# Two attention heads' blocks on one core: a periodic loop with its output group and VectorE's small work at one place in 16 steps

## Chip, cores, metric

One core of a Trainium2 chip runs the kernel. The metric is the device time in microseconds, as the median of several runs; before the change it is 1823.55 us (three runs, 1822.85 to 1823.87). "The loop" below is the main loop over 512 steps, in which nearly all the attention of block B is done.

## The reference

Two independent attention blocks over 2048 rows of 640 numbers, with 32 heads of 20 columns each; their outputs are put side by side. In A a row attends to eight keys, itself and seven before it, two apart; in B to all 2048.

```python
def _A_ref(x, wqkv, wo):
    ...
    logits = jnp.einsum("bhsd,bhswd->bhsw", q, kg) * scale
    logits = jnp.where(mask[None, None, :, :], logits, -1e9)
    attn = _softmax(logits, axis=-1)
    o = jnp.einsum("bhsw,bhswd->bhsd", attn, vg)
    return (lambda x, *d: x.transpose(*d))(o, 0, 2, 1, 3).reshape(B, S, D) @ wo

def _B_ref(x, wqkv, wo):
    ...
    scores = jnp.einsum("bhqd,bhkd->bhqk", q, k) * (Dh ** -0.5)
    p = _softmax(scores, axis=-1)
    o = jnp.einsum("bhqk,bhkd->bhqd", p, v)
    return (lambda x, *d: x.transpose(*d))(o, 0, 2, 1, 3).reshape(B, S, D) @ wo

return jnp.concatenate([a, b], axis=-1)
```

## The kernel before

The program is written out by Python in a fixed order: each engine has a wrapper `InOrder` (line 48) whose instructions keep the order in which they are written, so all work of an engine stands in one line of the profile, L60. A counter `now` is moved on by `tick()`, and `after(n, fn, ...)` puts work n ticks later. Ahead of the loop stand the projections of A and of B and the value groups of B; behind it the last output groups.

**Block B in the loop.** Four heads are worked on together (`g`, 8 of them), with 512 queries at a time (`qc`, 4); a unit `u` is one (g, qc), and it has 16 steps, one for each 128 keys. A step has four score matmuls ("s"; two heads in a plane `pl`, one in each row half `r` of TensorE's array), each followed by an exponential on ScalarE out of its PSUM bank (`e<-ps_st`), and the product of the exponentials of two steps earlier with V ("P", `b_pv`, four heads side by side in one bank). Two steps of P are summed in the bank; then ScalarE copies it (`more<-ps_st`), and GpSimd adds it to the unit's sum (`braw`).

The exponentials need the maximum of each query's row, which is taken out of the scores themselves by two additional rows of the operands. So the scores are computed a second time, transposed and 24 steps ahead (`LEAD`), as "m" matmuls, and VectorE takes the maximum out of PSUM (`mx<-ps_st`): a single one over 512 columns or a double one over two neighbouring banks, 1024 columns. A step has four m matmuls. At a unit's end `max_rows` reduces the sixteen columns on VectorE, transposes them, splits them on GpSimd and takes them through DRAM into the operand q. `normalize`, also at a unit's end, takes the sums through DRAM, a reciprocal on VectorE (`sm`), back through DRAM, and a product on GpSimd.

In the trace, an s matmul has 62 rows (`ps_st<-bq,bk 62*128`: a head's 20 columns three times, as high and low parts, and the two rows of the maximum), an m matmul 60 (`ps_st<-bk,bq 60*128`), and P is `ps_st<-e,vb`.

**The order of a pair of steps.** `b_pair` writes two steps at a time: P, then three couples of matmuls through `b_two`, P, and five couples, in the order P, s+m, m+m, s+s; P, s+m, m+m; s+s, s+m, s+m. Each couple uses both row halves of the array. m+m is read by one double maximum, the m of an s+m by a single one: two doubles and four singles per pair. Between the second and the third part of every third pair, an output group may stand. PSUM has eight banks (`psb`). Once the loop has begun, `one` and `two` choose a bank for each matmul when the program is written, out of the program's own account of when each bank has been read (`read_at`, `pe.us`, `act.us`, `dve.us`).

**Block A in the loop.** GpSimd does A's windows in 128 units (`a_attention`): per tile of 128 rows four units of scores, then `a_softmax` (a maximum and a reciprocal on VectorE, `am`, an exponential on ScalarE, the rest on GpSimd), then four units with V. In the loop a unit is written at 8 of 30 steps. A finished tile is turned by `a_turn`: VectorE transposes five blocks (`turn`), one a step, which go through DRAM and come back (`back`); `turn_parts` splits them on GpSimd. `a_out` then multiplies the tile by A's output weights: two output groups per tile, each of fifteen matmuls (`ps_st<-ww,aot`) into one bank, which ScalarE copies out (`ro`). 32 such groups stand in the loop. `fill` holds the output groups of B, which come up near the end.

Of the kernel before, what the change touches and what calls it, by code (L numbers as in the profile page):

```python
# [21 lines left out]
KC = 5  # L22
# [42 lines left out]
def attention_pair(ctx, tc, xa, wqk_a, wv_a, wo_a, xb, wqk_b, wv_b, wo_b, oa, ob):  # L65
# [16 lines left out]
    loop = [None]  # L82

# [14 lines left out]
    read_at = []  # L98

    def bank():  # L100
# [259 lines left out]

    def a_softmax(t):

        _, L, _ = a_t[t]
        if t % (NT // 2) == 0:
# [8 lines left out]
        yield  # L373
# [5 lines left out]
        yield  # L379
        dve.reciprocal(m[:, 0], m[:, 0])  # L380
        yield
        pool(L, L, m[:, 0].unsqueeze(1).to_broadcast([128, WIN, H]), ALU.mult)
# [17 lines left out]
    def a_attention():  # L400
        for n in range(2):
            a_fetch(n)
        soft = {}
        for n, (t, c) in enumerate(UNITS):
            a_fetch(n + 2)
            for g in soft.values():
                next(g, None)
            if c == 4:
                for _ in soft.pop(t):
# [12 lines left out]
            next_a[0] = n + 1  # L422
            yield
# [165 lines left out]
    def max_rows(m4, m1, q, qc):  # L589
# [5 lines left out]
        def turn():  # L595

            dve.transpose(raw, m1)

# [12 lines left out]
        t = odd(1)  # L611
        after(t, dve.tensor_reduce, m1[:, :16], m4.rearrange("p r a c -> p (r a) c"), AX.X, ALU.max)
        after(t, turn)
        after(t + 1, parts)
        after(t + 3, store)
        after(t + 4, load)

    def normalize(raw, g, c0, t, then):
# [9 lines left out]
        def out():  # L628
            for j in range(GH):
                r0 = (g * GH + j) * DH  # L630
                sp.dma_start(ot_b[r0:r0 + DH, c0:c0 + 512], raw[32 * j:32 * j + DH])
        after(t, sp.dma_start, s_d[0], raw[DH:128:32])
        after(t + 1, sp.dma_start, sm, s_d[0].rearrange("j (p c) -> j p c", c=16))
        t = odd(t + 3)
        after(t, dve.reciprocal, sm, sm)
        after(t + 1, sp.dma_start, s_d[1].rearrange("j (p c) -> j p c", c=16), sm)
        after(t + 2, bcast)
        after(t + 4, pool, raw, raw, rb, ALU.mult)
        after(t + 8, out)
        if then:  # L640
            after(t + 9, then)
# [6 lines left out]
    def max_tiles(i):  # L648
        u, sub = divmod(i, NKB)
        if sub == 0:  # L650
# [14 lines left out]
    def max_end(i):  # L665
        u, sub = divmod(i, NKB)
        if sub == NKB - 1:
# [45 lines left out]
    behind_v = [False]  # L713

    def b_pv(i):
# [38 lines left out]
    def b_two(what):  # L754

# [32 lines left out]
    def b_pair(i, pv):  # L788

        m = i + LEAD  # L790
        max_tiles(m)
        s = [("s", i + j, pl, r) for j in range(2) for pl in range(2) for r in range(2)]
        pv(i - LAG)
        b_two([s[0], ("m", m, 0, 1)])
        b_two([("m", m, 1, 0), ("m", m, 1, 1)])
        b_two([s[1], s[2]])
        yield
        pv(i - LAG + 1)
        b_two([s[3], ("m", m, 0, 0)])
        b_two([("m", m + 1, 0, 0), ("m", m + 1, 0, 1)])  # L800
        yield
        b_two([s[4], s[5]])
        b_two([s[6], ("m", m + 1, 1, 1)])
        b_two([s[7], ("m", m + 1, 1, 0)])
        max_end(m + 1)
# [53 lines left out]

    V_GROUPS = [(n, half, s) for n in (2, 3, 0, 1) for half in range(2) for s in range(4 * n, 4 * n + 4)]  # L860
    v_late = V_GROUPS[-LAG:]
    for n, half, s in V_GROUPS[:-LAG]:
# [17 lines left out]
        if groups in (26, 28):  # L880
            v_piece(0, *((0, 4) if groups == 26 else (8, 16)))
    tick()
    after(4, v_piece, 0, 4, 8)
    wait[0] = 2
    WO, loads = [], []

    def load_out(src, W, halves=range(2)):
        for h in halves:
            w, more = wide_pieces(src[h], gp)
            W.append(w)  # L890
            loads.extend(more)
    load_out(wo_a, WO, (0,))
    assert next(steps, None) is None

# [15 lines left out]
    for e in (pe, act, dve):  # L910
        e.us = 0.0
    for i in range(NS + LAG):
# [16 lines left out]
        if i + LEAD >= NS:  # L929

            read_at.clear()
            if i < NS:
                b_qk(i)
            if i % 2:
                b_pv(i - LAG - 1)
                b_pv(i - LAG)
                if fill:
                    fill.pop(0)()
            continue
        if i % 2 == 0:  # L940
            steps = b_pair(i, b_pv if i else lambda _: v_group(*v_late.pop(0)))
        next(steps)
        if i % 2 == 0:
            continue
# [4 lines left out]
        if fill:  # L949
            fill.pop(0)()  # L950
        elif i % 6 == 5 and not out_piece() and not left_a[0] and not WO_b:
            load_out(wo_b, WO_b)
        next(steps, None)
# [57 lines left out]
```

## Time and profile before

| | |
|---|---|
| median of three runs | 1823.55 us |
| span of the profiled execution, first to last instruction | 1820.8 us |
| TensorE / VectorE / ScalarE / GpSimd busy | 1802.5 / 1337.7 / 1327.9 / 1219.7 us |
| loop, from the first P to the 487th | 453.64 to 1712.79 us |
| mean granted TensorE clock | 0.998 |

The page gives the span of one profiled execution; its own time, launch included, is not listed, and the runs lie 2.1 to 3.1 us above the span. A line of a list in order of time has the start, the time for which the group was busy, engine, operation, tiles and count, and in brackets the idle time ahead of it with what ended it; equal instructions that follow each other closely are one line. A line of a stage table has the stretch, its length, and for TensorE, its weight loads, VectorE, ScalarE and GpSimd (those that have any) the busy time and count.

### The profile page before, as it was taken

The numbers are of one execution on the slowest core, as the hardware profiler recorded it, in microseconds if no ns is written. First come the engines' busy times: TensorE is split into PE (matmuls) and PEld (weight loads), VectorE is DVE, ScalarE is ACT, GpSimd is POOL, SyncE is SP. The second block draws the span as 40 slices with busy tenths as digits, with TensorE's granted clock in tenths as the row PEclk, the third lists the DMA queues.
The fourth block names the chain that finished last, engine by engine and source line by source line (L and its number), as shares of the span: only waits on it lengthen the run. The fifth ranks groups of instructions, "written<-read, shape, count | busy, mean of one in ns | idle before, by whom it ended". The sixth has DMA issues, their size and how long they took to land. (4 is left out here: it accounts for less than half of the span.)

```text
span 1820.8 us, 31714 instructions
## 1 busy us (share of the span) xinstructions
PE 1802.5 (99%) x11211; PEld 997.1 (55%) x11211; DVE 1337.7 (73%) x1838; ACT 1327.9 (73%) x2597; POOL 1219.7 (67%) x1072
## 2 busy tenths in 40 slices
PE   9999999999999999999999999999999999999999
PEld 8888888877344444444343444444444444443568
DVE  3100232357999999999999899999999999999400
ACT  4222322212998888998989889889998999899892
POOL 0000068856689889999989989899999973346232
PEclk9999999999999999999999999999999999999999
DMA  6323696874443444354435335353543441121023
GB/s 227 112 94 108 193 311 247 275 246 142 127 145 111 131 131 124 119 146 138 116 106 154 116 115 130 112 146 103 154 129 121 109 116 53 40 67 55 28 74 110
DMA packets 193015, 240.31 MB, mean 132 GB/s; under 512 B 90972, under 2 KB 121308, under 8 KB 191864
## 3 DMA queue, kind: packets, MB, share of 16 engines
q1 hardware_dynamic: 192280, 237.63, 43.1%
q8 instruction: 88, 1.44, 0.3%
q10 hardware_dynamic: 576, 0.66, 0.1%
q14 instruction: 71, 0.58, 0.1%
HBM read 173.29 MB, written 64.91 MB: 131 GB/s over the span
## 5 line engine op out<-in xcount | busy, mean ns | idle before, releaser
L60 DVE TENSOR_REDUCE mx<-ps_st 128x1 f32<-128x512 f32 (+1 forms) x1512 | 1216.0, 869 | 95.3 <-PE ps_st L60 92.1
L60 ACT ACTIVATE e<-ps_st 128x512 f32<-128x512 f32 x2048 | 1063.2, 611 | 54.6 <-PE ps_st L60 36.3
L60 PE MATMUL ps_st<-bq,bk 62*128 62x512 f32 x2048 | 629.4, 443 | 1.1 <-ACT e L60 0.5
L60 PE MATMUL ps_st<-bk,bq 60*128 60x512 f32 x2048 | 594.5, 441 | 7.5 <-DVE mx L60 4.2
L60 PEld LDWEIGHTS ps_st<-bq,bk 62*128 62x128 f32 x2048 | 286.1, 184 | 523.1 <-ACT e L60 296.7
L60 PE MATMUL ps_st<-e,vb 128*32 128x512 f32 x4096 | 542.9, 604 | 3.0 <-ACT e L60 2.8
L60 POOL TENSOR_TENSOR braw<-braw,more 128x512 f32<-128x512 f32 x224 | 287.6, 1284 | 199.6 <-ACT more L60 196.1
L60 POOL TENSOR_TENSOR akv<-akv,aq 128x1280 f32<-128x1280 f32 x64 | 189.0, 2953 | 239.5 <-DMA akv<-ka_d 239.5
L60 PEld LDWEIGHTS ps_st<-bk,bq 60*128 60x128 f32 x2048 | 273.6, 184 | 51.1 <-DVE mx L60 23.6
L60 POOL TENSOR_TENSOR akv<-akv 128x640 f32<-128x640 f32 (+3 forms) x304 | 284.5, 936 | 23.8
L60 ACT COPY ro<-ps_st 128x480 f32<-128x480 f32 (+1 forms) x124 | 61.3, 496 | 237.2 <-PE ps_st L60 182.7
L60 PEld LDWEIGHTS ps_st<-e,vb 128*32 128x32 f32 x4096 | 82.1, 108 | 159.4 <-issue 99.8
L60 POOL TENSOR_TENSOR akv<-akv,al 128x1280 f32<-128x1280 f32 x64 | 152.1, 2377 | 13.2 <-DMA bq<-qb_d 7.0
L60 PE MATMUL ps_st<-wc,xn 128*128 128x480 f32 x576 | 135.8, 380 | 0.2 <-ACT xn L60 0.2
L60 ACT COPY more<-ps_st 128x512 f32<-128x512 f32 x224 | 132.8, 593 | 2.0 <-PE ps_st L60 1.8
L60 PE MATMUL ps_st<-ww,xn 128*128 128x320 f32 x768 | 129.5, 319 | 1.6 <-ACT ww L60 1.1
L60 PEld LDWEIGHTS ps_st<-ww,xn 128*128 128x128 f32 x768 | 116.0, 192 | 23.3 <-ACT e L60 9.2
L60 PEld LDWEIGHTS ps_st<-wc,xn 128*128 128x128 f32 x576 | 107.9, 188 | 18.0 <-ACT xn L60 0.8
L60 PE MATMUL ps_st<-xn,w 128*128 128x512 f32 x480 | 115.8, 390 | 0.0
L60 PEld LDWEIGHTS ps_st<-xn,w 128*128 128x128 f32 x480 | 90.1, 188 | 19.3
L60 ACT CAST pr<-ps_st 128x512 fp32r<-128x512 f32 x40 | 23.6, 589 | 100.9 <-PE ps_st L60 100.9
L60 DVE TENSOR_TENSOR pr<-ps_st,pr 128x512 fp32r<-128x512 f32 x40 | 27.7, 692 | 91.4 <-ACT pr L60 91.4
(64 smaller groups left out, 995.8 us busy)
## 6 DMA issues: line engine op xcount, KB each, us to landing
akv<-ka_d SPq DMA_DIRECT2D x128, 320.0 KB
akv<-va_d SPq DMA_DIRECT2D x128, 320.0 KB
kb_d<-pr SPq DMA_DIRECT2D x20, 512.0 KB
qb_d<-pr SPq DMA_DIRECT2D x20, 512.0 KB
bk<-kb_d SPq DMA_DIRECT2D x16, 640.0 KB
bq<-qb_d SPq DMA_DIRECT2D x64, 160.0 KB
rb<-s_d SPq DMA_DIRECT2D x128, 64.0 KB
stg<-xb SPq DMA_DIRECT2D x12, 512.0 KB
```

The costliest lines, as they stand in the source:

```text
L60: return self.tc.keep_in_program_order(op(*a, **k))
```

## The change

Four things are moved. First, the pairs: a table of tokens, `PAIR`, replaces `b_pair`'s order. A normal pair is P, s+s, m+m, s+m; P, s+m, s+s, m+m, s+m, s+m. The pair at the middle of each unit (`BESIDE`, step 8 of 16) starts with an output group G and has its two P side by side. `b_pairs` takes scores and maxima from two running sequences, so that an s and an m of a couple always have different row halves. Second, an output group stands only there, one in 16 steps (two at the last two places); in the loop B's groups are written only once the pairs are over. Third, VectorE's small operations no longer stand where they come due but go into a list, `beside`, which is written out behind the group: A's maximum and reciprocal, the five turned blocks, the two operations that turn the unit's maxima, and the reciprocal of the unit's sums. Fourth, A's units come every 4 steps, the first tile is turned ahead of the loop (which also loads half of A's output weights three groups earlier), and the normalization starts two steps earlier.

```diff
+    beside = []
+    def small(us, op, *args):
+        t = dve.us
+        op(*args)
+        dve.us = t + us
...
     def bank():
         if read_at:
-            n = one(pe.us)
-            pe.us = max(pe.us, read_at[n]) + 2.2
+            n = one(pe.us + 0.2)
+            pe.us = max(pe.us + 0.2, read_at[n]) + 2.2
+            behind_v[0] = True
...
     def a_softmax(t):
...
+            after(3, beside.append, (go,))
+            yield
+            while not done:
+                if t in late:
+                    go()
+                else:
+                    yield
...
-        dve.tensor_reduce(m[:, 0], L.rearrange("p o h -> p h o"), AX.X, ALU.max)
-        yield
+        yield from placed(0.61, dve.tensor_reduce, m[:, 0], L.rearrange("p o h -> p h o"), AX.X, ALU.max)
+        if loop[0] is None:
+            yield
         pool(L, L, m[:, 0].unsqueeze(1).to_broadcast([128, WIN, H]), ALU.subtract)
         yield
-        yield
+        if loop[0] is None:
+            yield
         act.activation(L, L, AF.Exp, scale=SCALE)
...
-        dve.reciprocal(m[:, 0], m[:, 0])
-        yield
+        yield from placed(0.33, dve.reciprocal, m[:, 0], m[:, 0])
...
         for k in range(KC):
-            after(1 + k, dve.transpose, b[:, k], o[:, k * 128:(k + 1) * 128])
-        after(KC + 2, sp.dma_start, d, b.rearrange("p k c -> p (k c)"))
-        after(KC + 5, back)
+            small(0.27, dve.transpose, b[:, k], o[:, k * 128:(k + 1) * 128])
+        after(2, sp.dma_start, d, b.rearrange("p k c -> p (k c)"))
+        after(5, back)
...
+            small(0.17, dve.tensor_reduce, m1[:, :16], m4.rearrange("p r a c -> p (r a) c"), AX.X, ALU.max)
+            small(0.21, dve.transpose, raw, m1)
+            after(1, parts)
+            after(3, store)
+            after(4, load)
+        if loop[0] is None:
+            after(1, turn)
+        else:
+            beside.append((turn,))
...
-            normalize(raws.pop(u), g, qc * 512, 2 if last else 5, (lambda: out_last(qc)) if last else None)
+            normalize(raws.pop(u), g, qc * 512, 2 if last else 3, (lambda: out_last(qc)) if last else None)
...
+    PAIR = "P ss MM sm P sm ss MM sm sm".split()
+    BESIDE = "G ss sm MM sm P P ss sm MM sm".split()
+    def b_pairs(pv, group):
+        scores = ((i, pl, r) for i in range(NS - LEAD) for pl in range(2) for r in range(2))
+        maxima = ((m, j) for m in range(LEAD, NS) for j in range(2))
+        steps = iter(range(-LAG, NS))
+        half = []
+        for i in range(0, NS - LEAD, 2):
+            for t in BESIDE if i % NKB == NKB // 2 else PAIR:
+                if t == "P":
+                    yield
+                    pv(next(steps))
+                elif t == "G":
+                    group()
...
+    def group():
+        for _ in range(2 if now[0] - loop[0] > NS - 60 else 1):
+            out_piece()
+        flush()
...
-        if i > 14 and i % 30 % 4 == 1 and next(a_work, 0) == 0:
+        if i > 14 and i % 4 == 3 and next(a_work, 0) == 0:
...
-        if done_a and done_a[0][0] <= 0 and i % 8 == 7 and i > 14:
-            a_turn(*done_a.pop(0)[1:])
+        if i % NKB == NKB // 2 - 1 and done_a and done_a[0][0] <= 0:
+            beside.append((lambda d=done_a.pop(0): a_turn(*d[1:]),))
```

How this moves instructions, on VectorE first. In the middle of the loop before, around one turn of a tile (`turn`, `am` and `sm` as above; 128x1 is a single maximum, 128x2 a double):

```order
L60 TENSOR_REDUCE mx_7661<-ps_st 128x1 x2
L60 STREAM_TRANSPOSE turn<-ao 128x128
L60 TENSOR_REDUCE mx_7661<-ps_st 128x1
L60 TENSOR_REDUCE mx_7661<-ps_st 128x2
L60 STREAM_TRANSPOSE turn<-ao 128x128
L60 RECIPROCAL am<-am 128x32
L60 TENSOR_REDUCE mx_7661<-ps_st 128x1
L60 TENSOR_REDUCE mx_7661<-ps_st 128x2
```

And the place at which a tile is turned now:

```order
L60 TENSOR_REDUCE mx_8528<-ps_st 128x1 x2
L60 RECIPROCAL am<-am 128x32
L60 RECIPROCAL sm<-sm 128x16
L60 STREAM_TRANSPOSE turn<-ao 128x128 x5
L60 TENSOR_REDUCE mx_2532<-mx_8528 128x16
L60 STREAM_TRANSPOSE mtr<-mx_2532 128x32
L60 TENSOR_REDUCE mx_8981<-ps_st 128x1
L60 TENSOR_REDUCE mx_8981<-ps_st 128x2
L60 TENSOR_REDUCE mx_8981<-ps_st 128x1 x2
```

The nine small operations that stood singly among the maxima of several pairs follow each other at one place, between the last maximum of a unit and the first of the next. On TensorE, an output group before, in the middle of a pair (from a P to the next):

```order
L60 MATMUL ps_st<-e,vb 32x512 x4
L60 MATMUL ps_st<-bq,bk 128x512
L60 MATMUL ps_st<-bk,bq 128x512 x3
L60 MATMUL ps_st<-ww,aot 128x320 x15
L60 MATMUL ps_st<-bq,bk 128x512 x3
L60 MATMUL ps_st<-bk,bq 128x512
```

And now, from the last normal pair's end:

```order
L60 MATMUL ps_st<-ww,aot 128x320 x15
L60 MATMUL ps_st<-bq,bk 128x512 x3
L60 MATMUL ps_st<-bk,bq 128x512 x3
L60 MATMUL ps_st<-bq,bk 128x512
L60 MATMUL ps_st<-bk,bq 128x512
L60 MATMUL ps_st<-e,vb 32x512 x8
L60 MATMUL ps_st<-bq,bk 128x512 x3
```

The group moved from between two couples of a pair to a pair's start, and the two P of that pair (x4 each, now x8) moved behind four couples.

More of the change, by code (lines that the diff above doesn't have):

```diff
@@ L82, in attention_pair, with in_place @@
     loop = [None]
+    beside = []
[3 more added lines that the diff above has]
+        dve.us = t + us
+    def in_place(n, *ops):
+        if loop[0] is None:
+            for op in ops:
+                after(n, small, *op)
+        else:
+            after(n, beside.extend, ops)
     def odd(n):
@@ L378, in a_softmax @@
         pool(m[:, 0], m[:, 0], m[:, 1], ALU.add)
[L379 to L381 removed]
+        if loop[0] is None:
+            yield
+        yield from placed(0.33, dve.reciprocal, m[:, 0], m[:, 0])
+        if loop[0] is None:
+            yield
         pool(L, L, m[:, 0].unsqueeze(1).to_broadcast([128, WIN, H]), ALU.mult)
@@ L408, in a_attention @@
             if c == 4:
+                late.add(t)
                 for _ in soft.pop(t):
@@ L610, in load, with turn @@
                              md[:, r * 1024:(r + 1) * 1024].rearrange("t (p c) -> t p c", p=2))
[L611 to L616, printed above, removed]
+        def turn():
+            small(0.17, dve.tensor_reduce, m1[:, :16], m4.rearrange("p r a c -> p (r a) c"), AX.X, ALU.max)
[3 more added lines that the diff above has]
+            after(4, load)
+        if loop[0] is None:
+            after(1, turn)
+        else:
+            beside.append((turn,))
     def normalize(raw, g, c0, t, then):
@@ L631, in out, with turn @@
                 sp.dma_start(ot_b[r0:r0 + DH, c0:c0 + 512], raw[32 * j:32 * j + DH])
+        def turn():
+            small(0.24, dve.reciprocal, sm, sm)
+            after(1, sp.dma_start, s_d[1].rearrange("j (p c) -> j p c", c=16), sm)
+            after(2, bcast)
+            after(4, pool, raw, raw, rb, ALU.mult)
+            after(8, out)
+            if then:
+                after(9, then)
         after(t, sp.dma_start, s_d[0], raw[DH:128:32])
         after(t + 1, sp.dma_start, sm, s_d[0].rearrange("j (p c) -> j p c", c=16))
[L634 to L641, printed above, removed]
+        if now[0] - loop[0] < NS - LEAD - NKB // 2 - 4:
+            after(t + 3, beside.append, (turn,))
+        else:
+            after(t + 3, turn)
     mxt = {}
@@ L857, in v_group, with load_out @@
         after(1, sp.dma_start, vb_d[s * 128:(s + 1) * 128, half * 16 * VC:half * 16 * VC + c], ve[:, :c])
+    WO, loads = [], []
+    def load_out(src, W, halves=range(2)):
+        for h in halves:
+            w, more = wide_pieces(src[h], gp)
+            W.append(w)
+            loads.extend(more)
     V_GROUPS = [(n, half, s) for n in (2, 3, 0, 1) for half in range(2) for s in range(4 * n, 4 * n + 4)]
@@ L881, in attention_pair @@
             v_piece(0, *((0, 4) if groups == 26 else (8, 16)))
+        if groups == 14:
+            a_turn(*done_a.pop(0)[1:])
+        turn_parts()
+        if groups == 28:
+            wait[0] = 2
+            load_out(wo_a, WO, (0,))
+        if loads and groups >= 28:
+            loads.pop(0)()
     tick()
     after(4, v_piece, 0, 4, 8)
[L884 to L893, printed above, removed]
+    assert next(steps, None) is None and not loads
     outs = iter(())
@@ L911, in attention_pair, with flush @@
         e.us = 0.0
+    def flush():
+        while beside:
+            op = beside.pop(0)
+            (small if len(op) > 1 else op[0])(*(op if len(op) > 1 else ()))
+    def group():
+        for _ in range(2 if now[0] - loop[0] > NS - 60 else 1):
+            out_piece()
+        flush()
+    steps = b_pairs(lambda i: b_pv(i) if i >= 0 else v_group(*v_late.pop(0)), group)
+    next(steps)
     for i in range(NS + LAG):
@@ L948, in attention_pair @@
             spare += [sb.tile([128, 2, 512], F32, tag="last0", bufs=2, name="more") for _ in range(2)]
[L949 to L953, printed above, removed]
+        if i < NS - LEAD:
+            next(steps, None)
+            if not left_a[0] and not WO_b:
+                load_out(wo_b, WO_b)
+            continue
+        read_at.clear()
+        flush()
+        if i < NS:
+            b_qk(i)
+        if i % 2:
+            b_pv(i - LAG - 1)
+            b_pv(i - LAG)
+            if fill:
+                fill.pop(0)()
     qc = NQC - 1
```

80 lines of the change are left out of this document (39 added, 41 removed).

## The prediction

> **What bounds the kernel now.** I read the page first, then the stage table for the stretch of the main loop, then the engines' lists in order of time inside it. The page's first lines:
>
> ```profile
> span 1820.8 us, 31714 instructions
> PE 1802.5 (99%) x11211; PEld 997.1 (55%) x11211; DVE 1337.7 (73%) x1838; ACT 1327.9 (73%) x2597; POOL 1219.7 (67%) x1072
> ```
>
> TensorE looks full, but this is an average over stages, and a matmul that waits for a bank with its predecessor in flight shows no gap. The stage that counts is the periodic part of the loop. In the list of matmuls the first P times V starts at 453.64 us and the 487th at 1712.79: 486 steps, or 243 pairs. The stage table for that stretch, for all instructions and then for small tiles (turned rows of head block A, the turned maxima, the reciprocals of the sums, the softmax of A):
>
> ```profile
> 453.64:1712.79 1259.15, 1249.93 (x8311) 540.48 (x8310) 1189.10 (x1660) 1138.07 (x2241) 1019.31 (x890) 1.00 0.39 113
> ```
> ```profile
> 453.64:1712.79 1259.15, 23.45 (x80) 1.00 0.39 113
> ```
> ```profile
> 453.64:1712.79 1259.15, 6.56 (x31) 14.32 (x62) 1.00 0.39 113
> ```
> ```profile
> 453.64:1712.79 1259.15, 7.21 (x30) 1.00 0.39 113
> ```
> ```profile
> 453.64:1712.79 1259.15, 12.17 (x26) 33.30 (x66) 1.00 0.39 113
> ```
>
> The third column of busy time is VectorE: 1189.10 of 1259.15 us, 94%, ahead of ScalarE's 1138.07; the clock is granted in full (1.00). Now VectorE in order of time:
>
> ```profile
> 669.39 0.61 DVE L60 TENSOR_REDUCE am<-al 128x32 f32<-128x256 f32 x1
> 669.93 9.38 DVE L60 TENSOR_REDUCE mx<-ps_st 128x1 f32<-128x512 f32 x12
> 679.24 0.23 DVE L60 RECIPROCAL sm<-sm 128x16 f32<-128x16 f32 x1
> 679.40 0.15 DVE L60 TENSOR_REDUCE mx<-mx 128x16 f32<-128x64 f32 x1
> 679.58 0.21 DVE L60 STREAM_TRANSPOSE mtr<-mx 128x32 f32<-128x32 f32 x1
> 679.72 14.41 DVE L60 TENSOR_REDUCE mx<-ps_st 128x1 f32<-128x512 f32 x18
> 694.36 1.83 DVE L60 TENSOR_REDUCE mx<-ps_st 128x1 f32<-128x512 f32 x2 [0.22 <-PE ps_st L60]
> 697.66 1.29 DVE L60 TENSOR_REDUCE mx<-ps_st 128x1 f32<-128x512 f32 x2 [1.48 <-PE ps_st L60]
> 698.87 0.30 DVE L60 STREAM_TRANSPOSE turn<-ao 128x128 f32<-128x128 f32 x1
> 699.32 1.82 DVE L60 TENSOR_REDUCE mx<-ps_st 128x1 f32<-128x512 f32 x2 [0.15 <-PE ps_st L60]
> 701.06 0.30 DVE L60 STREAM_TRANSPOSE turn<-ao 128x128 f32<-128x128 f32 x1
> 701.28 2.98 DVE L60 TENSOR_REDUCE mx<-ps_st 128x1 f32<-128x512 f32 x4
> ```
>
> A pair has six maxima out of PSUM, four single and two double. The twelve from 669.93 are two pairs; the next instruction starts at 679.24, so two pairs take 9.31 us: **VectorE's floor is 4.655 us a pair**. Two singles take 697.66 to 698.87, 0.60 each (the second lasts 0.68 until it has landed), so a double takes 1.12. The small operations stand in the same queue, and from one start to the next they cost 0.54 (A's maximum), 0.16 (reciprocal of sums), 0.18 + 0.14 (the two that turn the maxima) and 0.22 (one turned block, 701.06 to 701.28). In the loop these are 80, 31, 30 and 26 instructions: 80 x 0.22 + 31 x 0.32 + 30 x 0.16 + 13 x 0.54 + 13 x 0.33 (A's reciprocal, for which I take its whole duration from the row quoted further down) = 43.6 us.
>
> The third piece of the loop is the output groups, fifteen matmuls in one bank. TensorE around the one at 694 us:
>
> ```profile
> 690.75 1.06 PE L60 MATMUL ps_st<-e,vb 128*32 128x512 f32 x8 [0.19 <-ACT e L60]
> 691.74 0.49 PE L60 MATMUL ps_st<-bq,bk 62*128 62x512 f32 x1
> 694.46 2.47 PE L60 MATMUL ps_st<-ww,aot 128*128 128x320 f32 x15
> 696.86 0.73 PE L60 MATMUL ps_st<-bq,bk 62*128 62x512 f32 x3
> 697.20 0.63 PE L60 MATMUL ps_st<-bk,bq 60*128 60x512 f32 x2
> 697.43 0.39 PE L60 MATMUL ps_st<-bq,bk 62*128 62x512 f32 x1
> 697.76 0.64 PE L60 MATMUL ps_st<-e,vb 128*32 128x512 f32 x4
> ```
>
> The group holds TensorE from 694.46 to 696.86, 2.40 us, in which no maximum is made; VectorE runs dry and stands for 1.48 us at 697.66. This pair takes 697.76 - 690.75 = 7.01 us, 2.36 over the floor. By the list of matmuls the loop has 35 such groups, 32 of A's output and three of B's near the end. In sum: 243 x 4.655 = 1131.2, small work 43.6, groups 35 x 2.36 = 82.6: 1257.4 against 1259.15 measured; the rest of 1.8 I carry over. So **nothing is hidden today**: VectorE pays for small work while it is the bound, and then stands idle at the groups.
>
> **The change part by part.** The number of matmuls, exponentials and maxima is unchanged, and so is the number per pair; what changes is where things stand.
>
> *Small work at the groups.* Every 16 steps one output group is issued, and all small operations that have come due stand in VectorE's queue right behind the last maximum ahead of it. Per period that is 0.32 + 0.16 us, and by turns A's reciprocal with five turned blocks (1.1) or A's maximum (0.54): about 1.9 and 1.0 us. The pause that they meet: VectorE still has 1.7 us of maxima when the group starts (694.46; the two from 694.36 end at 696.19), the group takes 2.40, the scores behind it 0.34 (696.86 to 697.20), and a maximum starts 0.46 after its matmul (697.20 to 697.66): 2.40 + 0.34 + 0.46 - 1.7 = 1.5 us, which is the row's 1.48. In the new pair two P times V follow each other and hold maxima back a second time; one P takes 0.99 (690.75 to 691.74), so for at most 0.9 us. Both ends: a group costs no less than 1.5 and no more than the 2.36 of now. I take 2.1 us, nearer to the row that has the whole cost, with the small work inside it, and keep 1.9 and 2.4 for the range. **The 43.6 us of small work go**, and 30 places cost 30 x 2.1 = 63.0. Two more groups stand second at the last two places, 2 x 2.40 = 4.8.
>
> *The other pairs.* P times V, two scores, double maximum. The order must keep VectorE fed, and two rings decide. In the built program the steady pair uses one couple of banks for both doubles, and its last single waits for the bank of its second. First ring: that single's read (0.68), score and maximum until P times V (697.43 to 697.76: 0.33), P to score (690.75 to 691.74: 0.99), score to double maximum (0.34), to the read (0.46): 2.80. VectorE meanwhile has the same read, a double and two singles: 0.60 + 1.12 + 1.20 = 2.92. It fits, with 0.12 to spare. The second ring goes through ScalarE:
>
> ```profile
> 545.89 1.06 PE L60 MATMUL ps_st<-e,vb 128*32 128x512 f32 x8
> 547.08 0.59 ACT L60 COPY more<-ps_st 128x512 f32<-128x512 f32 x1
> ```
> ```profile
> 1006.26 3.54 ACT L60 ACTIVATE e<-ps_st 128x512 f32<-128x512 f32 x7
> L60 ACT ACTIVATE e<-ps_st 128x512 f32<-128x512 f32 x2048 | 1063.2, 611 | 54.6 <-PE ps_st L60 36.3 <-ACT e L60 4.4
> ```
>
> Seven exponentials in 3.54 us, the last one lasting 0.61, are 0.49 from start to start. P to copy 1.19, copy 0.49, three exponentials 1.47, the fourth until its bank is free 0.61, scores and maxima 0.34 + 0.23, to P 0.33: 4.66 us, just at the floor. TensorE itself needs for a pair 2 x (0.99 + 0.33), a first slot of 0.34 behind each P and six of 0.23, less what overlaps: under 4.5. I take 4.70 a pair: the floor and a margin for ScalarE's extra work (A's exponential, the output's copy). The lower bound is 4.655, the upper one 4.80.
>
> *Moved with it.* A's units go from 8 in 30 steps to one in 4; GpSimd is 1019.31 of 1259.15 us busy now and gets no new work. The normalization's store and load are issued two steps earlier and its reciprocal stands two steps behind the load, as before; the store of the maxima is two steps earlier. SyncE's queue keeps its order within these chains. A's exponential now stands one unit behind GpSimd's subtraction instead of two; where GpSimd is late, ScalarE stands with all exponentials behind it. I take nothing for it, and as upper bound the longest wait for GpSimd's small tiles in the rows below, 1.1 us, at 15 tiles: 16 us, which the range holds. Half of A's output weights are loaded three groups earlier: no new work. Three of B's output groups, which now stand in the last pairs, come behind the loop: 3 x 2.40 = 7.2, on TensorE, which sets the end there (the last 107.99 us). The first turn of A moves ahead of the loop, into a stage in which VectorE has room; five blocks at 0.22 cost nothing there, or 1.1 us without that cover.
>
> A row that speaks on the collected queue:
>
> ```profile
> DVE sm L60 <- DMA sm<-s_d: 5.0, 2, 3.4
> DVE am L60 <- POOL am L60: 2.0, 2, 1.1
> L60 DVE RECIPROCAL am<-am 128x32 f32<-128x32 f32 x16 | 5.3, 330 | 2.0 <-POOL am L60 2.0
> ```
>
> VectorE stood behind late inputs of small work for 7.0 us in all, four times, with the small work spread out. [...]
>
> **Sum.** Ahead of the loop 453.6; pairs 243 x 4.70 = 1142.1; groups 63.0 + 4.8; the rest 1.8; so the loop 1211.7 against 1259.15. Behind it 108.0 + 7.2. Together 1780.5 of span, 40.3 less than now. The runs' median is 1823.55, 2.8 above the span that the profile gives; with that I forecast **1783 us**.
>
> **The rivals.** (1) *The floor is reached* and the pause is 1.9: 243 x 0.045 + 30 x 0.2 = 17 less, 1766. For it: the rings fit; against it: both are within 0.12 of the floor. (2) *A ring is longer than the floor.* The new order puts two scores before the first maximum behind P, so a late exponential holds up VectorE. At 4.80 a pair and 2.4 a group: 24 + 9 more, 1816. The gain is gone at 4.70 + 40.3/243 = 4.87 a pair; at 4.95, one missed slot of 0.25 in each pair, it is 61 more, **1844, slower**. Against: the two rings worked out, and the present order, whose pairs stay at the floor by the account above. (3) *The queue stands at the collected place.* Each place has about 0.7 us of pause left beyond the small work. If a reciprocal comes 2.5 us late (the mean of the two waits seen) at all 30 places, that costs 30 x 1.8 = 54, 1837; from 2.0 us on the gain is gone. [...] (4) *The change doesn't do what it says*: the small work was no cost, since the pause merely moves, and the groups keep 2.36 with the small work outside: 30 x 0.26 + 43.6 more, 1834 at 4.70 a pair, 1823 at 4.655: no gain. Against it the account, in which all three pieces add up.
>
> **How the numbers follow.** My forecast, with the values between 1773 and 1800, 0.55; rival 1 0.18; rival 2 0.16, two thirds of it still faster; rival 3 0.07; rival 4 0.04. The range of 8 in 10 is 1763 to 1815: rival 1 and a little under it below, the faster part of rival 2 above. What a measurement here can tell from no change is some 0.2%, 3.6 us. Faster by more than that 0.83, within it 0.04, slower 0.13.
>
> **What the profile afterwards would show.** VectorE's busy share over the periodic loop at 96% or more; stretches of six maxima at 4.66 to 4.72 us; the pause behind the group filled by the reciprocals and turns and no idle time over 1 us elsewhere; P times V of one pair to the next 4.70, about 6.8 with a group. Wrong would be: idle time of VectorE put down to TensorE in pairs without a group (rival 2), waits of VectorE for the sums' transfer or GpSimd above some 20 us (rival 3), or a pair with a group at over 8 us (rival 4).

## The result and the profile after

The changed kernel takes **1794.27 us** (median of four executions, 1791.18 to 1796.51), the kernel before 1823.20 beside it (1822.57 to 1823.87): a ratio of 0.984, 95% interval 0.9826 to 0.9854. That is 28.9 us less, where 40.5 were forecast; 1794 lies in the range, 11 us above the forecast. The page's first lines of the kernel after:

```profile
span 1791.9 us, 31505 instructions
...
PE 1776.2 (99%) x11211; PEld 985.1 (55%) x11211; DVE 1340.3 (75%) x1838; ACT 1325.5 (74%) x2597; POOL 1222.7 (68%) x1072
```

The work is the same and so are the busy times; the span is 28.9 us shorter. The stage table for the same 486 steps, first P to 487th, which now run from 454.31 to 1677.61 us:

```profile
454.31:1677.61 1223.30, 1218.00 (x8266) 522.66 (x8265) 1188.66 (x1655) 1135.07 (x2239) 1018.76 (x889) 1.00 0.41 115
```

VectorE has the same 1189 us of work in 36 us less: 97.2% instead of 94%. The loop takes 1223.3 against 1211.7 forecast, so **the whole miss of 11.6 us is in the loop**. Outside it the span has 568.6 against 561.6 before: 6.3 us more behind the loop, where 7.2 were forecast for B's three output groups, and 0.7 more ahead of it.

VectorE in order of time at one of the thirty groups (start, busy time, operation, tiles, count; idle time ahead in brackets):

```profile
862.70 7.72 DVE L60 TENSOR_REDUCE mx<-ps_st 128x1 f32<-128x512 f32 x10
870.35 0.34 DVE L60 RECIPROCAL am<-am 128x32 f32<-128x32 f32 x1
870.61 0.19 DVE L60 RECIPROCAL sm<-sm 128x16 f32<-128x16 f32 x1
870.72 1.02 DVE L60 STREAM_TRANSPOSE turn<-ao 128x128 f32<-128x128 f32 x5
871.66 0.18 DVE L60 TENSOR_REDUCE mx<-mx 128x16 f32<-128x64 f32 x1
871.87 0.21 DVE L60 STREAM_TRANSPOSE mtr<-mx 128x32 f32<-128x32 f32 x1
872.01 2.38 DVE L60 TENSOR_REDUCE mx<-ps_st 128x1 f32<-128x512 f32 x3
874.98 7.16 DVE L60 TENSOR_REDUCE mx<-ps_st 128x1 f32<-128x512 f32 x9 [0.60 <-PE ps_st L60]
```

From 870.35 to 872.01 stand nine small operations, 1.66 us, and VectorE is never idle for more than 0.04 us: this is the pause of 1.48 us of the kernel before, filled. Behind the two P that follow each other stand 0.60 us more. Together 2.26 us, against 2.1 taken. Two rows of the table of waits, over the whole span (total, times, longest), show what became of the idle time and of the fear of a late input (rival 3):

```profile
DVE mx L60 <- PE ps_st L60: 61.0, 82, 10.6
DVE sm L60 <- DMA sm<-s_d: 13.7, 2, 7.1
```

VectorE's waits for a score were 92.1 us before. The two waits for the sums lie at 1708.75 and 1751.46 us, behind the loop; inside it the collected queue never stood.

### Where the pair loses its last 0.06 us

Normal pairs take 4.71 to 4.72 us in the steady state. What holds them there is looked for in rings: closed chains, in which each instruction waits for the one before and the last one leads to the first one of the next pair. The list in order of time shows one, from P at 889.73 to P at 894.44, and the half behind it; first TensorE (matmuls, and two weight loads with what they waited for), then VectorE, then ScalarE:

```profile
889.73 1.06 PE L60 MATMUL ps_st<-e,vb 128*32 128x512 f32 x8
...
893.95 0.18 PEld L60 LDWEIGHTS ps_st<-bq,bk 62*128 62x128 f32 x1 [0.32 <-ACT e L60]
893.95 0.49 PE L60 MATMUL ps_st<-bq,bk 62*128 62x512 f32 x1
...
894.44 1.06 PE L60 MATMUL ps_st<-e,vb 128*32 128x512 f32 x8
...
895.44 0.49 PE L60 MATMUL ps_st<-bq,bk 62*128 62x512 f32 x2
...
895.77 0.40 PE L60 MATMUL ps_st<-bk,bq 60*128 60x512 f32 x2
...
896.02 0.39 PE L60 MATMUL ps_st<-bk,bq 60*128 60x512 f32 x1
...
896.34 1.06 PE L60 MATMUL ps_st<-e,vb 128*32 128x512 f32 x8
```
```profile
893.24 1.81 DVE L60 TENSOR_REDUCE mx<-ps_st 128x1 f32<-128x512 f32 x2
894.97 0.68 DVE L60 TENSOR_REDUCE mx<-ps_st 128x1 f32<-128x512 f32 x1
895.57 0.68 DVE L60 TENSOR_REDUCE mx<-ps_st 128x1 f32<-128x512 f32 x1
896.22 1.23 DVE L60 TENSOR_REDUCE mx<-ps_st 128x2 f32<-128x1024 f32 x1
```
```profile
892.82 0.58 ACT L60 COPY more<-ps_st 128x512 f32<-128x512 f32 x1
893.30 4.25 ACT L60 ACTIVATE e<-ps_st 128x512 f32<-128x512 f32 x8
897.52 0.59 ACT L60 COPY braw<-ps_st 128x512 f32<-128x512 f32 x1
```

**The ring through VectorE** (the prediction's first ring): the second single is read from 893.24 for 0.68 us, its bank goes to the couple at 893.95, which is 0.03 after the read ends; that couple holds P until 894.44, **0.49 us later**; P to score 1.00, score to the double maximum 0.33, to its read at 896.22 0.45. From 893.24 to 896.22 that is 2.98 us. VectorE's own work in between starts at 893.24 and its last single at 895.57 would let the next begin 0.60 later, at 896.17: 2.93. So VectorE stands 0.05 to 0.06 us in each pair, and 4.655 + 0.06 = 4.715 is the pair. The prediction had 2.80 for this ring, with 0.33 from couple to P. That 0.33 is right for a couple that finds its banks free (896.02 to 896.34 here: 0.32), but not for this one, which waited for its bank. The same holds in the whole loop: 0.33 us (median) where the last couple ahead of P follows the one before it within 0.3, and 0.49 where it comes 0.4 to 0.5 behind it.

**The ring through ScalarE**: copy at 892.82, exponential 0.48 later; 0.65 after that starts the couple at 893.95 (the weight load's row puts its wait down to an exponential); P 0.49 later, scores 1.00 later, the second P 0.90 later, and the copy at 897.52, 1.18 behind that P. The sum is 4.70, without VectorE in it. Two rings of nearly one length meet in the same couple, and VectorE's own sum lies just under them; which of them binds can't be read from this list. That took experiments.

### The profile page after: what moved, and what is told of

Same layout as the page of the kernel before. It is cut to its first block, busy times and chain, and to the rows that moved or that the text cites. A ratio compares the mean times of both kernels' runs of the same rounds, so it can differ in the third digit from the quotient of the medians.

```text
span 1791.9 us, 31505 instructions
## 1 busy us (share of the span) xinstructions
PE 1776.2 (99%) x11211; PEld 985.1 (55%) x11211; DVE 1340.3 (75%) x1838; ACT 1325.5 (74%) x2597; POOL 1222.7 (68%) x1072
## 4 chain that ended last, share of the span: by engine, by line
PE 87%; ACT 5%; DVE 4%; POOL 1%; DMA 1%; issue 1%; SPq 0%; POOLq 0%; ACTq 0%
PE ps_st L60 87%; ACT e L60 4%; DVE mx L60 4%; ACT more L60 1%; POOL akv L60 1%; DMA bq<-qb_d 1%; DMA stg<-wv_b 1%; POOL braw L60 0%; DMA mdr<-mtr 0%; SPq L60 0%; DVE xl L60 0%; ACT braw L60 0%; POOL ao L60 0%; POOL al L60 0%; DVE pr L60 0%
## 5 line engine op out<-in xcount | busy, mean ns | idle before, releaser
L60 DVE TENSOR_REDUCE mx<-ps_st 128x2 f32<-128x1024 f32 (+1 forms) x1512 | 1209.5, 872 | 61.9 <-PE ps_st L60 61.0
L60 ACT ACTIVATE e<-ps_st 128x512 f32<-128x512 f32 x2048 | 1059.4, 616 | 31.4 <-PE ps_st L60 12.3
L60 PE MATMUL ps_st<-bq,bk 62*128 62x512 f32 x2048 | 636.3, 455 | 2.3 <-DVE mx L60 0.6
L60 PE MATMUL ps_st<-bk,bq 60*128 60x512 f32 x2048 | 578.3, 431 | 4.8 <-DMA bq<-qb_d 3.8
L60 PEld LDWEIGHTS ps_st<-bq,bk 62*128 62x128 f32 x2048 | 276.3, 183 | 535.5 <-ACT e L60 366.1
L60 PE MATMUL ps_st<-e,vb 128*32 128x512 f32 x4096 | 536.7, 603 | 1.1
L60 PEld LDWEIGHTS ps_st<-bk,bq 60*128 60x128 f32 x2048 | 277.0, 185 | 21.5 <-DVE mx L60 11.6
```

What stands on the lines that cost most here:

```text
L60: return self.tc.keep_in_program_order(op(*a, **k))
```

## Experiments

In the expectations, letters stand for theories: **A** is the prediction's account, small work that vanishes into the pause behind the group. **B** puts the pair's excess down to the new order's rings, so that the old order would do better in the new loop. **C** is the two rings above, through VectorE's read and through ScalarE's copy. **D** is the number of PSUM banks that are free. Each kernel is the changed one with the edit shown. Ratios are to the kernel before, which took 1823.09, 1822.85 and 1822.84 us beside the three sets of runs; 0.984 is the change itself.

### Small work at another place (e1_place_apart)

```diff
     def group():
         ...
-        flush()
...
         tick()
+        if i % NKB == 10:
+            flush()
```

> The small work stays collected, but stands three steps behind the output group, in a normal pair. Theory A (the place behind the group hides it, because VectorE has nothing to do there): it costs its whole length again, 30 places x 1.45 us (the mean of 1.0 and 1.9) = 43.6 us, less what the 0.05 us of idle time per pair take up: 1828 to 1838 us, against 1794 with the change. Rival (collecting alone is what helps, or the small work costs nothing either way): within 5 us of 1794.

Measured 1840.34 us (1834.24 to 1852.38), 1.0103 [1.0065, 1.0142]: slower than before the change, and 46 us above it. VectorE at a group and at the place of the small work:

```profile
1140.16 2.42 DVE L60 TENSOR_REDUCE mx<-ps_st 128x1 f32<-128x512 f32 x3 [1.45 <-PE ps_st L60]
...
1145.54 0.34 DVE L60 RECIPROCAL am<-am 128x32 f32<-128x32 f32 x1
1145.80 0.20 DVE L60 RECIPROCAL sm<-sm 128x16 f32<-128x16 f32 x1
1145.91 1.02 DVE L60 STREAM_TRANSPOSE turn<-ao 128x128 f32<-128x128 f32 x5
1146.86 0.18 DVE L60 TENSOR_REDUCE mx<-mx 128x16 f32<-128x64 f32 x1
1147.07 0.21 DVE L60 STREAM_TRANSPOSE mtr<-mx 128x32 f32<-128x32 f32 x1
1147.21 3.55 DVE L60 TENSOR_REDUCE mx<-ps_st 128x2 f32<-128x1024 f32 x4
```

The pause is back (1.45 us) and the same small work, again 1.67 us, now pushes maxima back. The median lies 2 us above the range of A, far from the rival's 1794; the fastest execution, with a granted clock of 0.997, took 1834.24 and lies in it. So A holds: **the place is the gain, not the collecting.** The spread of the runs goes with a lower clock (0.983 in the slowest) and is told in the last section.

### The new pairs without the new place (e5_pairs_alone)

Groups in every third pair and small work where it comes due, as before, with the new order of the pairs.

```diff
-    BESIDE = "G ss sm MM sm P P ss sm MM sm".split()
+    PAIR_G = "P ss MM sm P sm ss MM G sm sm".split()
...
-            for t in BESIDE if i % NKB == NKB // 2 else PAIR:
+            for t in PAIR_G if (i + 1) % 6 == 5 else PAIR:
...
     def group():
-        for _ in range(2 if now[0] - loop[0] > NS - 60 else 1):
-            out_piece()
-        flush()
+        out_piece()
...
         tick()
+        flush()
```

(And the five turned blocks come one a step again.)

> The new order of the pairs alone: output groups in the fourth slot from the end of every third pair while there are any, as before, and the small work where it comes due. Theory A (all of the gain is the place of groups and small work): 1815 to 1830 us, no more than 0.5% from the kernel before. Rival (the order of the pairs is what gains): 1794 to 1805.

Measured 1826.13 us (ten executions, 1824.25 to 1828.81), 1.0018 [1.0009, 1.0027]. The order of the pairs by itself gains nothing.

### The old pairs in the new loop (e2_old_pairs)

```diff
-    PAIR = "P ss MM sm P sm ss MM sm sm".split()
+    PAIR = "P sm MM ss P sm MM ss sm sm".split()
```

> The order of the normal pairs as before (P, s+m, m+m, s+s; P, s+m, m+m; s+s, s+m, s+m) in the new loop, with the group and the small work at their new place. Theory B (the 4.71 us of a pair after the change come from the ring from a single's read through P and two scores to the next double, 2.97 us against VectorE's own 2.92): with s+m right behind P a maximum comes 0.34 us sooner, so the pairs are at the floor or up to 0.05 below 4.71: 1780 to 1794. Rival (the new order of the pairs is a gain of its own): 1800 to 1823.

Measured 1804.61 us, 0.9897 [0.9882, 0.9912]. B falls: the old order is no better, it is 10 us worse. By the starts of P in the trace its normal pairs take 4.77 us (median), with some at 5.0, against 4.72 in the new order. So the order is worth 10 us here and nothing in e5. In e5, by the same count, pairs without small work take 4.73 us (mean) and those with one or two small operations 5.02 and 5.09: the new pair is short only where no small work stands in it.

### More small work at the place (e3_more_small)

```diff
     def group():
         ...
         flush()
+        for k in range(KC):
+            small(0.27, dve.transpose, scrap, ident)
...
+    scrap = sb.tile([128, 128], F32, tag="scrap", bufs=1, name="scrap")
```

KC is 5, and nothing reads `scrap`.

> Five more transposes of 128x128 (5 x 0.22 = 1.1 us, of a tile that nothing reads) at each of the 30 places behind the group. Theory A (there is a pause of about 2.2 us there, and small work is free as far as it fits): the places that hold 1.0 us now have room, those that hold 1.9 come to 3.0 and run over by 0.8: 15 x 0.8 to 15 x 1.0 = 12 to 15 us, 1804 to 1811. Rival (the place is full): the whole 33 us, 1827. Other rival (VectorE is never what counts there): 1794 to 1797.

Measured 1810.03 us (1809.47 to 1811.02), 0.9931 [0.9917, 0.9946]: 15.8 us more for 30 x 1.1 = 33 us of added work. The pause still hides half of it, as A has it, and the time lies in A's range. But A had expected nothing at the places with little small work. By the starts of P, the second of the two pairs at such a place grows by 0.43 us (3.18 to 3.61) and at a full one by 0.98 (to 4.16), and the pair behind it gets 0.1 back. So the pause is somewhat shorter than the 2.2 us of the expectation, and at the full places the change has used it up.

### Shorter maxima (e4_max_448)

The maximum leaves out the last 64 of every 512 keys.

```diff
-    dve.tensor_reduce(..., psb[:, ns[0]:ns[0] + 2], AX.X, ALU.max)
+    dve.tensor_reduce(..., psb[:, ns[0]:ns[0] + 2, :448], AX.X, ALU.max)
...
-    dve.tensor_reduce(..., psb[:, n], AX.X, ALU.max)
+    dve.tensor_reduce(..., psb[:, n, :448], AX.X, ALU.max)
```

> In the loop VectorE takes the maxima over 448 of each 512 columns; the last 64 keys are left out of the maximum. VectorE's own sum for a pair falls by 4 x 0.067 + 2 x 0.133 = 0.53, from 4.655 to 4.12 us. Theory B (rings through P and the banks hold the pair): the ring loses only the 0.07 of one read, and ScalarE's ring of 4.66 stays: 0 to 17 us less than 1794, so 1777 to 1794. Rival (VectorE's sum is the bound): the pair falls to ScalarE's sum of 9 x 0.49 = 4.41, 243 x 0.30 = 73 us less, 1721.

Measured 1796.86 us, 0.9853 [0.9836, 0.9869]: no gain, 2.6 us above the change. Its stage table over the same 486 steps, and VectorE in order of time:

```profile
453.16:1682.39 1229.23, 1224.81 (x8267) 547.16 (x8265) 1087.81 (x1655) 1130.55 (x2238) 1019.00 (x889) 1.00 0.40 115
```
```profile
887.11 4.38 DVE L60 TENSOR_REDUCE mx<-ps_st 128x2 f32<-128x896 f32 x6 [0.36 <-PE ps_st L60]
891.85 4.37 DVE L60 TENSOR_REDUCE mx<-ps_st 128x2 f32<-128x896 f32 x6 [0.37 <-PE ps_st L60]
896.60 4.38 DVE L60 TENSOR_REDUCE mx<-ps_st 128x2 f32<-128x896 f32 x6 [0.37 <-PE ps_st L60]
```

VectorE has 101 us less to do and spends it waiting: six maxima in 4.38 us, then 0.36 idle, and the pair is still 4.74 (891.85 - 887.11). **Neither VectorE's sum nor the ring through its reads holds the pair by itself**, though VectorE was 97% busy.

### Shorter copies, alone and with shorter maxima (e9_copy_256, e10_copy_448)

```diff
-            act.copy(more, acc)
-            after(1, pool, raws[u], raws[u], more, ALU.add)
+            cols = slice(0, 256 if u < 30 else 512)
+            act.copy(more[:, cols], acc[:, cols])
+            after(1, pool, raws[u][:, cols], raws[u][:, cols], more[:, cols], ALU.add)
```

The copies and additions leave out half of these sums; e10 has this edit and that of e4.

> ScalarE copies, and GpSimd adds, 256 of the 512 columns of each sum but a unit's first (the other half of those sums is left out); no bank is held longer. Theory C (two rings of nearly one length, one through this copy, one through VectorE's single and double): the copy's ring falls by 0.2 us, the one through VectorE stays at 4.70: 0 to 12 us less, 1782 to 1794. Rival (the copy is what holds the pair): 210 pairs x 0.2 = 42 us less, 1752. Rival (banks and planner decide, whatever is shortened): within 5 of 1794 or slower.

> Both shortened: 256 columns in each copy and addition but a unit's first (the other half of those sums is left out), and maxima over 448 of 512 columns (the last 64 keys of each 512 are left out of the maximum). Theory C: with both rings shorter the pair falls to about 4.50: 210 x 0.2 = 42 us less than with one of them, 1740 to 1765. Rival (another limit, such as the banks in front of P, stands right behind): 1775 to 1795.

Measured: the copies alone 1795.17 us (1790.48 to 1796.54), 0.9845 [0.9832, 0.9858], the same as the change. Both together **1761.55 us** (1761.11 to 1762.93), 0.9668 [0.9653, 0.9682], 33 us less. VectorE in e10:

```profile
888.36 4.43 DVE L60 TENSOR_REDUCE mx<-ps_st 128x2 f32<-128x896 f32 x6 [0.30 <-PE ps_st L60]
892.99 4.38 DVE L60 TENSOR_REDUCE mx<-ps_st 128x2 f32<-128x896 f32 x6 [0.20 <-PE ps_st L60]
```

The pair is 892.99 - 888.36 = 4.63 here. Each edit alone gives nothing and the two together 33 us. That shows two limits of nearly one length behind each other: one goes away with shorter copies, the other with shorter maxima, as C has it. It does not show that the second one is a ring: 448 columns shorten the ring through the reads and VectorE's own sum alike, and no run separates the two. C's expectation for e9, 0 to 12 us less, was missed by 1 us. In e9's trace 69 of 180 normal pairs take 4.69 us or less (22 of 181 with the change alone), many of them 4.67 to 4.68, which is VectorE's sum within 0.03; others rise to 4.80, and the pair behind a place to 4.96 from 4.80 (medians). The edit of the copies also shortens GpSimd's additions (904 us of work in e10's loop instead of 1019), and that wasn't separated either. In e10 the pair was expected at 4.50 and is at 4.63, though the time lies in the range: a third limit stands there, and which it is stays open.

### Fewer copies (e7_four_steps, e8_four_448)

P is summed in its bank over four steps instead of two, which halves the copies; e8 adds the edit of e4.

```diff
-        n, part = divmod(kb, 2)
+        w = 4 if i < NS - 2 * NKB else 2
+        n, part = divmod(kb, w)
...
-                      start=(part == 0), stop=(part == 1))
+                      start=(part == 0), stop=(part == w - 1))
...
-        if part == 0:
+        if part < w - 1:
```

> P times V is summed in the bank over four steps instead of two, so every other copy and addition goes (steps 480 to 511 stay as they are). Theory C (ring through the copy): pairs without a copy lose that ring but keep the one through VectorE's single and double, 4.70: 0 to 12 us less, 1782 to 1794. Rival (ScalarE's sum is the bound): half of 0.48 us in each of 243 pairs, 58 us less, 1736. Other rival (a bank held over four steps is one bank fewer for scores): 1800 to 1830.

> Both: sums over four steps, and maxima over 448 of 512 columns (the last 64 keys of each 512 are left out of the maximum). Alone, the shorter maxima gave 1797. Theory C (two rings at nearly the same length, one through VectorE and one through the copy): only together do they let the pair go, by 0.15 to 0.3 us: 1720 to 1760. Rival (TensorE and the banks hold the pair whatever the two do): 1780 to 1797.

Measured 1840.42 us, 1.0092 [1.0076, 1.0109], and 1840.28, 1.0098 [1.0083, 1.0113]. C missed both by far: half the copies cost 46 us, and shorter maxima don't change that. The rival of e7, a bank that is held longer is a bank less for scores and maxima, had the sign right and too small a size. By the starts of P in e7, pairs in which a copy stands keep about 4.70 us, those without one take 5.00, and the two pairs at a place 12.3 instead of 11.6: the loss is where a bank is held through the pair. That fits this rival but doesn't prove it, since the planner (the program's choice of a bank for each matmul) may choose other banks here. e8 adds that shorter maxima don't win the loss back.

### Other orders of the pair (e6_single_first, e11_even)

```diff
-    PAIR = "P ss MM sm P sm ss MM sm sm".split()
+    PAIR = "P sm ss MM P sm ss MM sm sm".split()   (e6)
+    PAIR = "P ss MM sm sm P ss MM sm sm".split()   (e11)
```

> A third order of the normal pairs: P, s+m, s+s, m+m; P, s+m, s+s, m+m, s+m, s+m. VectorE gets a maximum right behind each P, as in the order before, and ScalarE two more scores right behind it. Theory C (a ring without VectorE holds the pair at 4.70 to 4.72: the copy of a sum, an exponential, the bank of the last couple, P, three couples, P, copy): all its terms are in this order too, so 1790 to 1806. Rival (theory B, the ring through the double maximum): that ring falls by 0.2 or more, and the pairs go to the floor of 4.655, 13 us less: 1781.

> A fourth order of the normal pairs, with nothing left out: both steps alike, P, s+s, m+m, s+m, s+m. Three couples stand ahead of each P in place of two and four, so fewer filled banks are in front of P in one step and more in the other. Theory C/D (eight banks; a couple waits for the last bank ahead of P, and P then starts 0.47 us behind it in place of 0.33): the waiting couple stands ahead of both P, twice 0.14 and twice the ring: 1800 to 1840. Rival (the uneven steps are the loss): 1780 to 1790, a version better than the change.

Measured 1906.47 us, 1.046 [1.0445, 1.0476], and 1836.94, 1.0078 [1.0066, 1.0091]. e6 was expected between 1781 and 1806 by one view or the other and both missed, by 100 us: median pair 5.43. For e11 the expectation of a slower pair held (4.93) and its rival, an even order that gains, fell. The rings worked out for one order do not carry over to another. A likely reason is that the planner then gives other banks to each matmul; no run shows it. None of these orders beats the change, and no kernel here that does the whole work does.

## Why the prediction was right, and where it was off

**The sign, and most of the size, came from the account of the loop before:** small work costs its length there and would go into the pause. That is what happened (no more than 0.04 us of idle time in 870.35 to 872.01), and e1 shows that it is the place which does it. e3 shows the limit: the full places have no room left.

**That the account closed to within 1.8 us was partly luck.** By the starts of P in the kernel before, its 130 pairs with neither small work nor a group took 4.72 us (median), not 4.655, and its 24 pairs with a group and no small work 6.88, so 2.16 more and not 2.36. The pairs were put some 15 us too low (243 x 0.06) and the groups 7 too high (35 x 0.20), which leaves 37 us for small work and the rest, where the prediction had 45. Its own rows point there: the twelve maxima at the floor stand right behind small work, when VectorE has a backlog; the eighteen from 679.72 begin at the same rate but last until 694.36, which is 4.88 a pair. By the same count the loop now has 8 us in place of the 37, and the difference of 29 is the measured gain. Pair and group cost what they had cost: 4.72 before and after, 2.16 and 2.17. So rival 2's "against", that the present pairs stay at the floor, did not hold.

**Groups at 2.1.** By the starts of P, the two pairs at a place take 11.60 us together (median), 2.17 over two of 4.715. The term was nearly right, but not as a gain over before. The sign "a pair with a group at over 8 us" can't be read as it was put: with the two P side by side, the starts of P give 8.42 and 3.18 for the two pairs.

**Behind the loop 7.2** was 6.3.

**TensorE's own sum.** The prediction's terms, as they stand, give 4.70 and not "under 4.5"; they count six slots of 0.23 where the list has four. With four they give 4.24, so TensorE wasn't the limit, and pairs of 4.57 in e10 agree. Its 1218.00 busy us of the loop's 1223.30 don't speak against that: the couple at 893.95, which waited, started 0.49 behind the one before it, where 0.25 lie between 895.77 and 896.02, and its row shows no gap.

**Rival 3, the queue that stands,** did not come in the loop. Its price, an estimate, was read from the wrong place: of the four waits in its rows, three lie outside the loop before (302.48, 1744.49 and 1786.98 us), both waits for the sums among them. In the one wait inside it VectorE kept the program's order: the reciprocal at 1470.16 stood for 1.13 us, and the maximum behind it, whose matmul had started at 1468.35, was read at 1470.43. With the change no small operation in the loop was late.

**The pair was mis-sized: 4.70 taken, 4.74 in the mean of the normal pairs** (starts of P, without those at a group and two long ones near the end). It has three parts. The steady pair is 4.715: the term that failed is the first ring, "2.80 ... with 0.12 to spare". Measured it is 2.98, for 0.16 more from a couple that had waited to P and 0.03 for handing the bank over. Since the ring through the copy has nearly the same length, how much of the excess is due to either stays open. The excess makes 243 x 0.015 = 3.6. The pair behind a group takes 4.80, 30 x 0.085 = 2.6. And every second period one pair takes 4.92, where A's exponential stands between ScalarE's exponentials and the copy. ScalarE in one of them:

```profile
923.75 4.25 ACT L60 ACTIVATE e<-ps_st 128x512 f32<-128x512 f32 x8
927.87 0.43 ACT L60 ACTIVATE al<-al 128x256 f32<-128x256 f32 x1
928.18 0.60 ACT L60 COPY more<-ps_st 128x512 f32<-128x512 f32 x1
```

The copy comes 0.31 us later for it, in 13 pairs, 13 x 0.2 = 2.6: the margin of the prediction named it, without a sum. Two pairs near the end take 6.39 and 7.27, 4.2 above the steady pair, where 1.8 was carried over as the rest: 2.4 more. The sum is 3.6 + 2.6 + 2.6 + 2.4 = 11.2 of the 11.6 us; the rest is at the groups, within the rounding of these figures.

**"VectorE's floor" was nearly right as a number, and it was not the whole cause.** 4.655 lies 0.06 under the pair. The prediction said that a ring decides if it is longer than the floor (rival 2, at 4.80 and more); a ring through the copy was, by some 0.05. The prediction had this second ring at 4.66 by one path; it is 4.70 by another that also goes through the waiting couple. e4 shows what follows: less work for VectorE alone gains nothing here; e9 and e10 show that it counts once the copy is shorter.

**What stays open.** That the pairs of e2, e6, e7 and e11 are longer is measured, but no run separates the order from the banks that the planner gave it. Whether VectorE's sum or the ring through its reads is the second limit of the pair is open. Why the pair behind a group takes 4.80 wasn't tried either.

## What to carry to other kernels

Small work of a nearly full engine is worth placing, not only collecting: put it into the pause that another stage makes anyway, and stop when the pause is full (1.66 us of work in 1.5 to 2.2 us here). When an engine is at 97% and its stage's floor is within 2% of the time (4.655 of 4.715 us a pair here), look for rings through the buffers before making that engine faster, add up each ring with the durations of instructions that *waited*, and shorten all limits of one length together. Check a floor on pairs that have no backlog in front of them, and each term of an account by itself: a sum that closes can hide errors that cancel. The order of the work around a full engine can be worth nothing before such a move and 10 us after it, so test parts in both settings.

## What the runs showed of the hardware

**A couple that waited held the next P longer.** From the last couple of matmuls to P took 0.32 us where the couple's banks were free and 0.49 where it had waited (rows of the kernel after, 896.02 and 893.95).

**A stall of 1.5 us, then half the clock.** e1's profiled execution is the slowest of its four (mean granted clock 0.983, 1852.38 us; the fastest, at 0.997, took 1834.24). TensorE in order of time, and the stage table with the granted clock in the third column from the end:

```profile
978.35 0.50 PE L60 MATMUL ps_st<-bk,bq 60*128 60x512 f32 x2 [1.51 <-ACT e L60]
...
979.25 1.76 PE L60 MATMUL ps_st<-e,vb 128*32 128x512 f32 x8
```
```profile
973.20:979.30 6.10, 4.59 (x36) 1.61 (x39) 6.07 (x16) 4.93 (x10) 3.29 (x5) 1.00 0.40 131
979.30:982.00 2.70, 2.70 (x15) 0.94 (x13) 2.02 (x3) 1.25 (x3) 2.62 (x2) 0.54 0.72 209
982.00:985.00 3.00, 3.00 (x12) 0.49 (x9) 1.82 (x2) 1.41 (x3) 2.69 (x6) 0.50 0.23 63
985.00:987.20 2.20, 2.20 (x18) 1.53 (x18) 1.25 (x2) 1.89 (x4) 2.20 (x3) 0.70 0.75 119
```

With the small work at that place TensorE stands for 1.51 us; right behind it the granted clock is 0.50 to 0.54, P takes 1.76 instead of 1.06, and the pair 7.86 us. In this execution TensorE stood for more than a microsecond twelve times in the loop, and eight of the stalls were followed by such a pair, of which seven took 7.8 us and one 6.6. The same pair behind the other four stalls took 5.47 at the full clock, so the lower clock cost 7 x 2.36 + 1.17, some 18 us by estimate. Without it this execution would lie near 1834, which is what the fastest one took and within the range that e1 was expected in. The stalls that the lower clock followed were 1.0 to 1.5 us long. That the stall causes it was not tested by itself, and four stalls of the same lengths (1.02 to 1.52 us) were not followed by it.

**Summing in one bank over four steps cost more than the copies that it saved.** With P's bank held over four steps the kernel took 46 us longer, though ScalarE had half the copies (e7); that the held bank is the reason fits the trace and isn't shown.
